# One transposition moved from a transfer to TensorE, one cast from ScalarE to VectorE, and other products cut in halves

## The chip, the cores and the metric

The kernel runs on one core of one Trainium2 chip. The metric is the device time of one execution in microseconds; lower is better. The core has five engines that run side by side and wait for each other by semaphores: TensorE (PE in the profile, its weight loads PEld), VectorE (DVE), ScalarE (ACT), GpSimd (POOL) and SyncE (SP). SyncE does no arithmetic: it issues transfers, in the order of the program. POOL issues transfers too, and each engine works its own list of instructions strictly in order.

## What is computed

A retention layer (attention with a decaying mask and no softmax) feeds a two-layer network with the Mish function. The reference, cut to what matters:

```python
# q, k, v: 8 batches x 8 heads x 576 positions x 64
scores = q @ k.T / sqrt(64)
gamma = 1 - 2 ** (-5 - head)
ret = (scores * where(i >= j, gamma ** (i - j), 0)) @ v
x = ret.transpose(0, 2, 1, 3).reshape(4608, 512)
h = x @ w_in                      # 512 -> 2048
g = h * tanh(softplus(h))         # Mish
out = g @ w_out                   # 2048 -> 512, float32
```

## The kernel before

The 4608 rows are cut into chunks of 128 positions of one batch (positions 512 to 575 of two batches share a chunk). There are 36 chunks; four make a tile of 512 columns, so there are nine tiles, t = 0 to 8. Chunks 0 to 7 (tiles 0 and 1) are the first 128 positions of each batch and go a way of their own. From chunk 8 (`N0`) on, each batch is worked through by running states: the sum of all earlier k-by-v products, kept per batch.

Each chunk from 8 on goes through these steps:

- `load(n)` (lines 266 to 281): POOL issues the transfers of q, k and v into `qkraw` (5 buffers) and `vraw` (7 buffers).
- `step_p(n)`, called "P" (line 291): two VectorE multiplications scale q and k by the decay and write `qks` in bf16.
- `step_v(n)`, "V" (line 298): v is scaled, on VectorE below chunk 18, on POOL from there on.
- `step_t(n)`, "T" (lines 301 to 319): q and k of the chunk are transposed into `qkT`. Below chunk `NPE` = 16, TensorE does it with eight 128x128 transposes into PSUM (line 310) and ScalarE copies the result out (line 316). From chunk 16 on, SyncE issues one transposing transfer (line 318).
- `step_s` (line 330), the scores of a pair of chunks, TensorE; `step_m` (line 336), the masking, VectorE.
- `states(n)` (line 385), the k-by-v products of a pair; `sum_up` (lines 408 to 416) adds them up on VectorE, and a cast to bf16 (line 419) waits in the list `casts` until `run(casts)` is called.
- `outputs` and `outputs_end` (lines 439 and 456), the retention's results; `outputs_copy` (line 468) brings them into the tile `xT`.

`visit(n)` does the TensorE part for a pair: the states and the scores of chunks n+2 and n+3, mixed with the outputs of chunks n and n+1. It is a stretch of 64x64 products, many instructions in a short time. `written` puts a waiting instruction on SyncE in the middle of each visit, so that transfers that SyncE issues later stand behind it.

The large products fill the time between visits. `g1(t, f)` makes one 128x512 block of the first layer (four products, line 504, and ScalarE's Mish, line 518, out of two PSUM buffers `hp`); `g2(t, i)` makes four products of the second layer. `product` (lines 502 to 510) does one such product as a whole, or, while the counter `halved[0]` is above zero, as two halves of 256 columns with a weight load each (line 509); the first and the last product of a sum are never halved.

The order of all this is written out by hand. A loop over u = 0 to 23 does the first layer of tile 1 and part of its second layer, with the steps of chunks 8 to 13 placed at fixed u. Then a loop over t = 2 to 9 and i = 0 to 15 goes on. In it, n = 4(t+1) + 2(i // 8) is the pair in work and w = i % 8 is the unit in its stage; below, "stage 14, unit 5" means n = 14 and w = 5. The visit of a pair stands in unit 6 of its stage. So tile 2 has stages 12 and 14, tile 3 has stages 16 and 18, and so on.

Transposing transfers and loads share the DMA engines. `hold(n)` (line 474) keeps them apart: POOL copies one element out of the transposed chunk n, so POOL, and every load behind it in POOL's list, waits until that transposition has landed. In stage 12 the lines around the change are:

```python
            if w == 7 and n + 4 == NPE:
                att(n + 5, "T")
                hold(n + 4)
                hold(n + 5)
                more_loads(n + 7)
```

Here `att(17, "T")` issues the transfer of chunk 17, the two holds wait for chunks 16 and 17, and `more_loads` goes on to chunk 18. Chunk 16 is transposed in unit 5 of stage 12. Chunks 18 and 19 are transposed, by transfers, in unit 7 of stage 14 and unit 0 of stage 16; visit 14 reads the scores' inputs of chunks 16 and 17, visit 16 those of chunks 18 and 19. In stage 14 the scaling "P" of chunk 18 stands in unit 4 and that of chunk 19 in unit 7.

Of the kernel before, what the change touches and what calls it, by code (L numbers as in the profile page):

```python
# [16 lines left out]
def kernel(  # L17
# [18 lines left out]
    nc = tc.nc  # L36
    B, H, S, D = q.shape
    assert (B, H, S, D) == (8, 8, 576, 64)
    P = 128
# [6 lines left out]
    NPE = 16  # L46
# [213 lines left out]
    def cast_k0(b, copy=nc.scalar.copy):  # L260
        k0[b] = first.tile([P, H, D], BF16, name="k0", bufs=3)
        copy(k0[b], k0r[b])
# [3 lines left out]
    def load(n):  # L266
        if n >= n_chunks:
            return
        b, c = chunks[n]
        qkr = io.tile([P, 2, H, D], F32, name="qkraw")  # L270
        vr = io.tile([P, H, D], F32, name="vraw", bufs=7)
        live[n] = {"qkr": qkr, "v": vr}
        for t, src in ((qkr[:, 0], q), (qkr[:, 1], k), (vr, v)):
            if c < 4:
                nc.gpsimd.dma_start(  # L275
                    out=t, in_=src[b, :, ds(P * c, P), :].rearrange("h p d -> p h d"))
            else:
                for e in range(2):
                    nc.gpsimd.dma_start(
                        out=t[ds(64 * e, 64)],  # L280
                        in_=src[b + e, :, ds(512, 64), :].rearrange("h p d -> p h d"))
# [19 lines left out]
    def step_t(n):  # L301
        flat = live[n]["qks"].rearrange("p i h d -> p (i h d)")
        qk = tr.tile([P, 2, NP, P], BF16, name="qkT", bufs=6)
        if n < NPE:
            if n in (N0 + 2, N0 + 4):
                tp = ps_st.tile([P, 2 * NP, P], BF16, name="st")
            else:
                tp = ps_sc.tile([P, 4 * NP, P], BF16, name="sc")[:, 0:2 * NP]
            for i in range(2 * NP):
                nc.tensor.transpose(tp[:, i, :], flat[:, ts(i, P)], ident)  # L310
            if n < N0 + NCH:

                nc.scalar.copy(qk[:, 0], tp[:, 0:NP])
                later.append(lambda: nc.scalar.copy(qk[:, 1], tp[:, NP:2 * NP]))
            else:
                nc.scalar.copy(qk.rearrange("p i n t -> p (i n) t"), tp)
        else:
            nc.sync.dma_start_transpose(out=qk.rearrange("p i n t -> p (i n) t"), in_=flat)
        live[n]["qk"] = qk
# [23 lines left out]
    def flush():  # L343
        while later:
            later.pop()()
# [6 lines left out]
    casts = []  # L352

    def behind(ins, others):

        sync = mybir.DependencyInfo(mybir.DependencyClass.Sync, mybir.DependencyReason.DATA)
        tc.add_manual_dep(ins.ins, others.ins.name, sync, reason="row halves and a bank")
# [8 lines left out]
    def states(n):  # L366

        if n >= n_chunks:
            return [], 0
        st = ps_sc.tile([P, 2, 2, NP, 64], F32, name="sc")  # L370
        whole = [b for b, c in chunks[n:n + 2] if c == 1]
        s0 = ps_st.tile([P, 2, NP, 64], F32, name="st")[:, 0] if whole else None

        made = []

        def part(x, j, p):
            r = ds(64 * j, 64)
            for e in range(2):
                hh = 4 * (p // 2) + 2 * e + p % 2
                if x is None:  # L380
                    ks, vs, to = k0[whole[0]][r, hh, :], v0s[whole[0]][r, hh, :], s0[ds(64 * e, 64), p, :]
                else:
                    ks, vs = live[n + x]["qks"][r, 1, 2 * p + e, :], live[n + x]["vs"][r, hh, :]
                    to = st[ds(64 * e, 64), j, x, p, :]
                ins = nc.tensor.matmul(to, lhsT=ks, rhs=vs, start=(x is not None or j == 0 and p == 0),  # L385
                                       stop=True, skip_group_check=True)
                made.append(ins)

        own = [x for x in range(2) if chunks[n + x][1] < 4]
        first_half, second_half = [None] * len(whole) + own, own + [None] * len(whole)  # L390

        def unit(i, seen=None):
            made.clear()
            for p in range(NP):
                part(first_half[i], 0, p)
                part(second_half[i], 1, p)
            if seen is not None:
                behind(made[0], seen)
            return made[-4:]

        def sum_up():
            new = tr.tile([P, 5, NP, 64], F32, name="total", bufs=2)
            lows = tr.tile([P, 5, NP, 64], BF16, name="ssb", bufs=2)
            k = 0
            for x in own:
                b, c = chunks[n + x]
                if c == 1:
                    nc.vector.tensor_copy(new[:, k], s0)
                    total[b], st_sb[b, c, 0] = new[:, k], lows[:, k]
                    k += 1  # L410
                for j in range(2):
                    if (c, j) == (3, 1):
                        st_sb[b, 4] = tr.tile([P, NP, 64], BF16, name="last", bufs=4)
                        nc.vector.tensor_tensor(st_sb[b, 4], st[:, j, x], total[b], op=OP.add)
                        continue
                    nc.vector.tensor_tensor(new[:, k], st[:, j, x], total[b], op=OP.add)  # L416
                    total[b], st_sb[(b, c, 1) if j == 0 else (b, c + 1, 0)] = new[:, k], lows[:, k]
                    k += 1
            casts.append(lambda: nc.scalar.copy(lows[:, 0:k], new[:, 0:k]))  # L419

        sums.append(sum_up)
        return [lambda seen=None, i=i: unit(i, seen) for i in range(len(first_half))], len(own)

    def run(jobs):
        while jobs:
            jobs.pop()()

# [42 lines left out]
    def hold(n):  # L472

        nc.gpsimd.tensor_copy(held[:, n % 2:n % 2 + 1], live[n]["qk"][:, 1, NP - 1, P - 1:P])  # L474
# [23 lines left out]
    halved = [0]  # L498
# [76 lines left out]
    def att(n, steps):  # L575
        if n >= n_chunks:
            return
        for step in steps:
            {"P": step_p, "V": step_v, "T": step_t}[step](n)

    dve, act, pool = nc.vector.tensor_copy, nc.scalar.copy, nc.gpsimd.tensor_copy
# [63 lines left out]
    for i in range(nF):  # L645
        for step in steps.get(i, "").split():
            n = int(step[1])
# [17 lines left out]
    def more_loads(upto):  # L665
        for _ in range(2):
            if queued[0] <= upto:
                load(queued[0])
                queued[0] += 1
# [5 lines left out]
    for u in range(24):  # L675
        j, w = divmod(u, 4)
        if u == 5:
            cast_k0(0)
        elif u == 14:
            cast_k0(1, dve)  # L680
        halved[0] = 2 if u < 5 else 0
        if u in ps:
            att(N0 + ps[u], "P")
        if u == 11:
            step_m(N0)
        if u in vs:
            att(N0 + vs[u], "V")
        if w == 0 and j > 0:
            if j < 5:
                if j == 4:  # L690
                    load_k0(2)
                load(N0 + j + 3)
            else:
                more_loads(N0 + j + PF)
                load_k0(3)
        if u == 10:
            units, early = states(N0)
            seen = written(units[0]())
            step_s(N0)
            units[1]()  # L700
            units[2](seen)
            run(sums)
        elif u == 16:
            att(N0 + 4, "P")
            visit(N0, ((ps_o, "ops"), (ps_h, "hp")), (act, act))
            run(sums)
        elif u == 22:
            visit(N0 + 2, ((ps_h, "hp"), (ps_h, "hp")), (act, dve))
        if u == 20:
            stores(act)  # L710
        if u in (13, 20):
            run(casts)
        if u in ts_:
            att(N0 + ts_[u], "T")
        stores()
        if u < nF:
            g1(1, u)
            flush()
        else:
            g2(1, u - nF)  # L720
# [3 lines left out]
    for t in range(2, nT + 1):  # L724
        for i in range(nF):
            n, w = NCH * (t + 1) + i // 8 * 2, i % 8
            if w == 2 and n in cast_at:
                cast_k0(cast_at[n])
            if w == 2:
                run(casts)  # L730
                halved[0] = {14: 10, 20: 24, 22: 24}.get(n, 0)
            if w == 6 and n < n_chunks:
                visit(n, ((ps_h, "hp"), (ps_h, "hp")), (act, dve), lambda: g2(t - 1, i))
            if w == 0:
# [3 lines left out]
                stores()  # L738
            if w in (0, 1) and n + 2 < NPE:
                att(n + 2 + w, "P")  # L740
            if w in ((4, 7) if n + 2 == NPE else (4, 5)) and n + 4 >= NPE:
                att(n + 4 + (w > 4), "P")
            if w in ((3, 4) if n + 2 < NPE else (0, 1)):
                att(n + 2 + (w in (1, 4)), "V")
            if w == 5 and 16 <= n < 24:
                f_state(1, n // 2 - 8, nc.vector)


            if w == 7 and n + 4 == NPE:
                att(n + 5, "T")  # L750
                hold(n + 4)
                hold(n + 5)
                more_loads(n + 7)
            if w == 4 and NPE < n + 2 < n_chunks:
                hold(n + 2)
                hold(n + 3)
# [69 lines left out]
```

## Time and profile before

| What | Value |
|---|---|
| median of three runs | 308.64 us (308.0 to 310.39) |
| the profiled execution's own time | 305.89 us |
| its span, first to last instruction | 304.2 us |
| mean granted TensorE clock | 0.994 |
| TensorE busy | 290.3 us, 95% of the span |
| VectorE, ScalarE, POOL busy | 135.4, 134.2, 137.9 us |
| transposing transfers | 20, landing 3.0 to 12.2 us after issue |

The profile is one execution. A group or timeline row names start and length in us, the engine, the line of the kernel, what is written and read, the shape and a count; the square bracket at the end tells how long the engine had stood idle before the row and what ended that wait. "issue" there means that no semaphore explains the wait. A row with SPq or POOL DMA is the issue of a transfer, not the transfer; a row "held<-qkT" on POOL is one `hold`. In the stretches, the busy time of each engine is followed by its number of instructions, then the granted clock, the mean share of time in which the 16 DMA engines were busy (it can pass 1, since packets overlap) and what they moved.

### The profile page before, as it was taken

Reading aid. Unit: us, or ns where it says so; the run is one execution under the profiler, and the core shown is the slowest. Engines: PE = TensorE matmul, PEld = TensorE weight load, DVE = VectorE, ACT = ScalarE, POOL = GpSimd, SP = SyncE. Lnnn points to the kernel's source line nnn. Section 1 sums busy time; section 2 is a strip of 40 time slices with the busy share of each in tenths; the row PEclk is TensorE's granted clock in tenths of the full one; section 3 lists DMA queues with packets and bytes.
Section 4 is the critical chain, followed back from the end, with each engine's and each line's share of the span. In section 5 each row is a group of like instructions: output and inputs, shape, how many; then the busy total and the mean of one; then the engine's idle time right before and its main releaser. Section 6 shows DMA issues by size and latency. Waiting matters only on the chain.

```text
span 304.2 us, 7939 instructions
## 1 busy us (share of the span) xinstructions
PE 290.3 (95%) x3456; PEld 159.5 (52%) x3494; DVE 135.4 (45%) x233; ACT 134.2 (44%) x220; POOL 137.9 (45%) x186
## 2 busy tenths in 40 slices
PE   8889999999989997999999999999899999999996
PEld 3456887555455543456656454545354544444443
DVE  3812547587963752554555545444443312011011
ACT  5656226785656532534353535343435343433300
POOL 8595856768408906591929345919240000000000
PEclk9999999999999997999999999999999999999999
DMA  7999999999986996989898989888922100110132
GB/s 150 204 206 205 205 241 230 333 220 204 253 158 168 213 163 177 217 194 190 190 194 135 198 170 228 183 166 152 196 72 69 39 34 34 37 34 34 37 102 71
DMA packets 41730, 47.96 MB, mean 158 GB/s; under 512 B 23904, under 2 KB 30560, under 8 KB 41696
## 3 DMA queue, kind: packets, MB, share of 16 engines
q0 software_dynamic: 14896, 32.25, 51.0%
q1 hardware_dynamic: 26656, 15.01, 24.0%
q8 instruction: 27, 0.44, 0.7%
q10 hardware_dynamic: 144, 0.20, 0.2%
q14 instruction: 7, 0.06, 0.1%
HBM read 38.80 MB, written 9.44 MB: 159 GB/s over the span
## 4 chain that ended last, share of the span: by engine, by line
PE 88%; DMA 6%; issue 2%; POOL 2%; ACT 1%; DVE 0%; POOLq 0%
PE hp L504 38%; PE ops L504 28%; PE hp L509 7%; PE ops L509 4%; DMA qkT<-qks 4%; DMA gT<-in_v_dram 2%; PE sc L330 2%; PE sc L385 1%; PE hp L456 1%; PE hp L559 1%; PE hp L439 1%; POOL gT L106 1%; PE st L509 1%; PE sc L310 1%; PE st L385 1%
## 5 line engine op out<-in xcount | busy, mean ns | idle before, releaser
L504 PE MATMUL hp<-xT,w_in_t 128*128 128x512 bf16 x495 | 127.3, 380 | 3.1 <-issue 1.1
L518 ACT ACTIVATE gT<-hp 128x512 bf16<-128x512 f32 x144 | 86.2, 599 | 96.0 <-PE hp L504 91.6
L504 PE MATMUL ops<-w_out_t,gT 128*128 128x512 bf16 x399 | 99.7, 381 | 2.0 <-issue 1.9
L504 PEld LDWEIGHTS <-w_in_t 128*128 128x128 bf16 x512 | 50.0, 98 | 54.8 <-issue 3.4
L504 PEld LDWEIGHTS <-gT 128*128 128x128 bf16 x468 | 44.7, 98 | 52.2 <-issue 2.0
L567 DVE COPY res<-ops 128x512 f32<-128x512 f32 x28 | 19.3, 691 | 79.8 <-PE ops L504 76.9
L291 DVE TENSOR_TENSOR qks<-qkraw,gqk 128x512 bf16<-128x512 f32 x56 | 36.9, 702 | 12.6 <-DMA qkraw<-in_k_dram 12.6
L474 POOL COPY held<-qkT 128x1 bf16<-128x1 bf16 x20 | 6.1, 304 | 71.4 <-DMA qkT<-qks 71.4
L468 DVE CAST xT<-hp 128x512 bf16<-128x512 f32 x13 | 9.0, 692 | 35.8 <-PE hp L456 33.1
L275 POOL DMA_DIRECT2D qkraw<-in_q_dram x24 | 21.4, 892 | 4.2 <-DMA vpair<-in_v_dram 1.5
L275 POOL DMA_DIRECT2D qkraw<-in_k_dram x24 | 21.2, 885 | 2.7 <-DMA w_out_t<-in_moe_w_out_dram 1.5
L275 POOL DMA_DIRECT2D vraw<-in_v_dram x24 | 21.2, 885 | 2.6 <-DMA vpair<-in_v_dram 1.5
L468 ACT CAST xT<-hp 128x512 bf16<-128x512 f32 x14 | 8.2, 587 | 31.6 <-PE hp L456 29.2
L509 PEld LDWEIGHTS <-gT 128*128 128x128 bf16 x184 | 17.6, 98 | 3.8
L298 POOL TENSOR_TENSOR vs<-vraw,gv 128x512 bf16<-128x512 f32 x18 | 18.9, 1077 | 1.2 <-PE hp L439 1.1
L509 PE MATMUL hp<-xT,w_in_t 128*128 128x256 bf16 x128 | 19.2, 272 | 0.0
L336 DVE TENSOR_TENSOR sm<-sc,mask 128x1024 bf16<-128x1024 f32 x14 | 17.0, 1216 | 1.4 <-PE sc L330 1.4
L416 DVE TENSOR_TENSOR total<-sc,total 128x256 f32<-128x256 f32 x40 | 16.9, 422 | 1.1
L509 PEld LDWEIGHTS <-w_in_t 128*128 128x128 bf16 x128 | 12.5, 98 | 7.7
L419 ACT CAST ssb<-total 128x768 bf16<-128x768 f32 (+3 forms) x14 | 12.9, 923 | 1.8 <-DVE total L416 1.7
L509 PE MATMUL ops<-w_out_t,gT 128*128 128x256 bf16 x100 | 13.1, 273 | 0.1
L504 PE MATMUL hp<-w_out_t,gT 128*128 128x512 bf16 x49 | 12.1, 379 | 0.1
(117 smaller groups left out, 249.7 us busy)
## 6 DMA issues: line engine op xcount, KB each, us to landing
out_dram<-res SPq DMA_DIRECT2D x31, 256.0 KB, 3.3
qkraw<-in_q_dram POOLq DMA_DIRECT2D x24, 256.0 KB, 6.9
qkraw<-in_k_dram POOLq DMA_DIRECT2D x24, 256.0 KB, 7.7
vraw<-in_v_dram POOLq DMA_DIRECT2D x24, 256.0 KB, 7.9
w_out_t<-in_moe_w_out_dram POOLq DMA_DIRECT2D x4, 512.0 KB, 11.7
k0r<-in_k_dram POOLq DMA_DIRECT2D x8, 256.0 KB, 5.5
w_in_t<-in_moe_w_in_dram POOLq DMA_DIRECT2D x3, 512.0 KB, 10.0
gT<-in_k_dram POOLq DMA_DIRECT2D x8, 128.0 KB, 6.4
```

Source lines behind the costliest of these rows:

```text
L275: nc.gpsimd.dma_start(out=t, in_=src[b, :, ds(P * c, P), :].rearrange("h p d -> p h d"))
L291: nc.vector.tensor_tensor(slots[:, :, y], heads[:, :, y], factors[:, :, y].unsqueeze(3).to_broadcast([P, NP, 2, D]), op=OP.mult)
L298: engine.tensor_tensor(vs, live[n]["v"], gv[:, c, :].unsqueeze(2).to_broadcast([P, H, D]), op=OP.mult)
L336: nc.vector.tensor_tensor(sm.rearrange("p e x n i -> p (e x n) i"), live[n]["sc"].rearrange("p e x n i -> p (e x n) i"), mask.unsqueeze(1) ...
L416: nc.vector.tensor_tensor(new[:, k], st[:, j, x], total[b], op=OP.add)
L419: casts.append(lambda: nc.scalar.copy(lows[:, 0:k], new[:, 0:k]))
L468: copy(xts[t][:, :, ds(P * s, 2 * P)].rearrange("p h (x j i) -> p j h x i", x=2, j=2)[:, j], both[j])
L474: nc.gpsimd.tensor_copy(held[:, n % 2:n % 2 + 1], live[n]["qk"][:, 1, NP - 1, P - 1:P])
L504: nc.tensor.matmul(to, lhsT=w, rhs=x, start=first, stop=last)
L509: nc.tensor.matmul(to[:, ts(j, n)], lhsT=w, rhs=x[:, ts(j, n)], start=False, stop=False, skip_group_check=True)
L518: nc.scalar.activation(gts[t][:, f, :], hp, AX.Mish)
L567: copy(ot, ops)
```

## The change

Four things are edited.

- `step_t` transposes chunk 17 on TensorE with a copy by ScalarE; chunk 16 and those from 18 on still go by transfers.
- The steps of chunk 17 are placed later: "P" in unit 2 of stage 14 (before: unit 5 of stage 12), "T" in unit 5 of stage 14 (before: unit 7 of stage 12). `hold(17)` is gone from stage 12.
- The waiting casts take the copying engine as an argument. At u = 13 it is VectorE (tile 2's first states, 128x1280); everywhere else it is ScalarE as before.
- The counter of halved products is set to 2 at u = 5 and 6 too, to 6 instead of 10 in stage 14, to 28 instead of 24 in stage 20, and to 10 instead of 24 in stage 22.

```diff
     def step_t(n):
...
-        if n < NPE:
+        if n < NPE or n == NPE + 1:
...
-            casts.append(lambda: nc.scalar.copy(lows[:, 0:k], new[:, 0:k]))
+            casts.append(lambda copy: copy(lows[:, 0:k], new[:, 0:k]))
...
-    def run(jobs):
+    def run(jobs, *how):
         while jobs:
-            jobs.pop()()
+            jobs.pop()(*how)
...
-        halved[0] = 2 if u < 5 else 0
+        halved[0] = 2 if u < 7 else 0
...
         if u in (13, 20):
-            run(casts)
+            run(casts, dve if u == 13 else act)
...
             if w == 2:
-                run(casts)
-                halved[0] = {14: 10, 20: 24, 22: 24}.get(n, 0)
+                run(casts, act)
+                halved[0] = {14: 6, 20: 28, 22: 10}.get(n, 0)
...
-            if w in ((4, 7) if n + 2 == NPE else (4, 5)) and n + 4 >= NPE:
+            if n + 2 == NPE and w == 2:
+                att(n + 3, "P")
+            if w in ((4, 7) if n + 2 == NPE else (4, 5)) and n + 4 >= NPE and (n + 4 > NPE or w == 4):
                 att(n + 4 + (w > 4), "P")
...
             if w == 7 and n + 4 == NPE:
-                att(n + 5, "T")
                 hold(n + 4)
-                hold(n + 5)
                 more_loads(n + 7)
+            if w == 5 and n + 2 == NPE:
+                att(n + 3, "T")
```

In the program that results, TensorE has 8 transposes more and 10 halved products fewer; VectorE's list has one cast more, ScalarE's one cast less and one copy of 128x1024 more, SyncE's one transfer less and POOL's one held copy less.

## The prediction

> **What bounds the kernel now.** The page comes first: where the time is, and who ends last.
>
> ```profile
> span 304.2 us, 7939 instructions
> ...
> PE 290.3 (95%) x3456; PEld 159.5 (52%) x3494; DVE 135.4 (45%) x233; ACT 134.2 (44%) x220; POOL 137.9 (45%) x186
> ...
> PE 88%; DMA 6%; issue 2%; POOL 2%; ACT 1%; DVE 0%; POOLq 0%
> ```
>
> TensorE is busy for 95% of the span and the other engines for half of it. So only two things can move the end: TensorE's own work, and the few places where it stands still. The second view is the chain that ended last, in order of time. DMA has 6% of it, and one piece stands in the middle of the kernel:
>
> ```profile
> 84.37 0.45 PE sc L310 x8
> ...
> 89.58 3.45 PE hp L504 x16
> ...
> 95.63 0.87 PE ops L509 x8
> ...
> 105.21 11.06 DMA qkT<-qks
> 117.61 1.49 PE ops L504 x3
> 119.10 2.20 PE hp L504 x8
> 121.30 0.86 PE ops L504 x4
> ```
>
> A transfer transposition issued at 105.21 us ends 11 us later, and TensorE goes on behind it. The third view is the timeline of TensorE around its visits (the stretches of 64x64 products). I quote the first row of the visits of chunks 12 and 16, and each row in them ahead of which TensorE stood still:
>
> ```profile
> 86.47 0.22 PE L385 MATMUL st<-v0s,k 64*64 64x64 bf16 x2
> ...
> 88.13 0.22 PE L330 MATMUL sc<-qkT 64*64 64x64 bf16 x3 [0.68 <-issue]
> ...
> 113.33 0.22 PE L385 MATMUL st<-v0s,k 64*64 64x64 bf16 x2
> ...
> 115.58 0.32 PE L330 MATMUL sc<-qkT 64*64 64x64 bf16 x16 [1.53 <-DMA qkT<-qks]
> ...
> 116.32 0.32 PE L330 MATMUL sc<-qkT 64*64 64x64 bf16 x16 [0.42 <-DMA qkT<-qks]
> ```
>
> Both visits hold the same kinds of work (with a k0 state). Visit 12 goes from 86.47 to 89.58, 3.11 us with a stall of 0.68, so 2.43 without; eight products (0.86 per four) then end at 4.2 us from its start. Visit 16 starts at 113.33 and its eight products end at 121.30: 7.97 us. Its two waits, 1.53 and 0.42 us, for the transposed chunks 18 and 19 explain half of the **3.8 us** lost. The rest is the clock, as the stretch behind the visit shows (columns: TensorE, its weight loads, DVE, ACT, POOL, granted clock, DMA share, GB/s):
>
> ```profile
> 118.00:120.50 2.50, 2.50 (x9) 0.97 (x8) 0.92 (x1) 0.03 (x1) 2.50 (x4) 0.61 0.65 161
> ```
>
> At 0.61 of the clock a product takes 0.27 to 0.5 us (rows 119.10 and 117.61 of the chain) instead of 0.22. The stall costs twice: while it lasts, and after it.
>
> **Why chunks 18 and 19 come late.** The queues' timeline and the stretches by DMA load:
>
> ```profile
> 83.96 4.69 SPq L318 DMA_TRANSPOSE qkT<-qks  x2
> ...
> 88.77 0.19 POOL L474 COPY held<-qkT 128x1 bf16<-128x1 bf16 x1 [9.09 <-DMA qkT<-qks]
> ...
> 92.32 0.54 POOL L474 COPY held<-qkT 128x1 bf16<-128x1 bf16 x1 [3.36 <-DMA qkT<-qks]
> ...
> 92.82 0.89 POOL L275 DMA_DIRECT2D qkraw<-in_q_dram  x1
> ...
> 103.30 7.34 SPq L318 DMA_TRANSPOSE qkT<-qks  x2
> ...
> 104.37 0.69 POOL L279 DMA_DIRECT2D vraw<-in_v_dram  x1 [0.26 <-DMA qkraw<-in_q_dram]
> ```
> ```profile
> 90.00:94.00 4.00, 4.00 (x21) 1.82 (x19) 3.34 (x7) 2.73 (x5) 1.68 (x3) 1.00 0.19 70
> 94.00:104.00 10.00, 9.79 (x178) 6.01 (x179) 4.87 (x8) 4.61 (x9) 10.00 (x13) 1.00 0.92 214
> 104.00:107.00 3.00, 3.00 (x16) 1.35 (x15) 1.79 (x6) 2.38 (x4) 2.72 (x4) 1.00 1.05 200
> 107.00:110.00 3.00, 3.00 (x15) 1.35 (x14) 1.29 (x3) 1.19 (x2) 0.12 (x1) 1.00 1.41 225
> ```
> ```profile
> DMA to landing us min/median/max: 3.0/5.9/12.2
> ```
>
> POOL's held(16) passes at 88.77; held(17) waits another 3.36 us for chunk 17's transfer, and only then, at 92.82, does POOL issue the loads of chunks 18 to 21. Meanwhile the DMA engines idle (share 0.19 from 90 to 94). The loads then fill them until about 109. Transpositions 18 and 19 are issued at 103.30 and 105.21, into full engines, and take 12.2 (the longest of all 20) and 11.1 us where the median is 5.9.
>
> **The change part by part.** The profiled execution took 305.89 us, its span 304.2, and the median shown is 308.64, or 2.75 above it; I take differences on the profile and subtract them from the median.
>
> *Chunk 17 off the transfer queue, held(17) gone.* SyncE and POOL each lose one instruction. held(16) waits only for chunk 16, issued at 83.96, 3.5 us ahead of 17, so it still passes at 88.77 and the next POOL instruction comes 3.55 us earlier (92.32 less 88.77), or 3.8 with the longer copy. All twelve loads' issues are back to back, so all move: the engines drain near 105.5 instead of 109. Transposition 18 stays at 103.3, since it stands on SyncE behind a result store that TensorE and DVE release. It then meets engines that drain 2 us later. With the median 5.9 us it lands at 109.2, and 19, issued at 105.2, at 111 to 113. TensorE asks for them at about 114.5 (113.33, plus the first units, plus 0.45 below). Both waits go, and with them the clock loss: **3.8 us** at most, 0 at least if the 12.2 us do not shrink. I take 3.8, because the slack is 1 to 3 us.
>
> *Chunk 17 on TensorE.* Eight transposes: 0.45 us on the chain (row 84.37 above), with nothing to hide them: **+0.45**. Their input, DVE's pair for chunk 17, moves from unit 5 of stage 12 to unit 2 of stage 14, behind the two value scalings of this row; ACT's copy and the scores that read chunk 17 follow:
>
> ```profile
> 84.94 1.02 ACT L316 COPY qkT<-sc 128x1024 bf16<-128x1024 bf16 x1
> ...
> 92.12 1.28 DVE L298 TENSOR_TENSOR vs<-vraw,gv 128x512 bf16<-128x512 f32 x2
> ...
> 99.56 0.50 PE L330 MATMUL sc<-qkT 64*64 64x64 bf16 x32
> ```
>
> The pair takes 1.28 us as well and ends near 94.7, unit 5 begins some 2.5 us ahead of the scores, near 97, and the copy, of 1.02 us, ends near 98.8, ahead of the scores at 99.56 plus 0.45. It delays one ACTIVATE by 1.02 us, behind which visit 14's second bank waits; TensorE has a unit of products in between. Cost 0; without that cover up to 0.6. The raw buffer that DVE now frees later is chunk 22's, loaded behind held(18) only.
>
> *The cast of 128x1280 from ACT to DVE.* The rows around unit 14 of stage 1:
>
> ```profile
> 64.22 1.27 ACT L419 CAST ssb<-total 128x1280 bf16<-128x1280 f32 x1
> ...
> 65.26 0.42 DVE L262 CAST k<-k0r 128x512 bf16<-128x512 f32 x1
> ...
> 66.04 1.02 PE L504 MATMUL hp<-xT,w_in_t 128*128 128x512 bf16 x4 [0.65 <-ACT gT L518]
> ...
> 67.92 0.20 PEld L330 LDWEIGHTS <-qkT 64*64 64x64 bf16 x14 [0.18 <-issue]
> ```
>
> ACT's 1.27 us stands ahead of the ACTIVATE that TensorE awaits for 0.65 us; that wait goes. On DVE the cast takes 0.42 (the 512 columns' row) to 1.05 us (0.42 x 1280/512; I take 1.0), and the k0 cast ends at 66.7 instead of 65.7, where the visit, at 66.99 now, would want it at 66.3. So 0.3 is left of 0.65. Behind it TensorE stops at 67.92 for its own code (next part), and that moment may not move. Bounds 0 and 0.65; I take **-0.2**.
>
> *Halves.* Eight halves take 0.87 us (95.63), four whole products 0.86 (121.30). Units 5 and 6 add four halved products, stage 14 loses four, 20 gains four, 22 loses fourteen: ten fewer, -0.03 us. What they change is the place of every later instruction. Three stops marked "issue" inside or behind visits have no semaphore; the weight loads up to them count:
>
> ```profile
> 0.00:88.10 88.10, 82.93 (x1106) 52.65 (x1118) 51.21 (x96) 51.79 (x85) 57.85 (x81) 1.00 1.08 222
> 0.00:216.05 216.05, 206.00 (x2753) 119.03 (x2782) 116.80 (x204) 105.87 (x173) 134.31 (x181) 0.99 0.98 198
> 0.00:67.91 67.91, 63.66 (x725) 41.75 (x734) 36.11 (x70) 39.70 (x67) 47.50 (x69) 1.00 1.09 222
> ```
> ```profile
> 216.09 0.38 PE L504 MATMUL hp<-xT,w_in_t 128*128 128x512 bf16 x1 [1.13 <-issue]
> ```
>
> 1118, 2782 and 734 differ by 384 and 1664 pairs of weight load and product: 3 and 13 times 128. So the code arrives in blocks of 256 instructions, and TensorE stops where a block comes late because a visit ran through the one before. In the new order the visits up to 12 lie 4 pairs later, 14 and 16 lie 8 later, 18 and 20 8 and 12, the later ones 0 to 2 earlier. The stop of 0.68 shrinks by up to four products' time (block asked for 0.87 us earlier), that of 1.13 by two (0.43): I take **-0.3 and -0.2**; bounds together are -1.8 (both gone) and +0.8 (a block needed 28 pairs, 6 us, behind visit 14 instead of 7.8 comes late).
>
> By the Trainium skill's "Runtime: NRT & Kernel Launch", section Instruction fetch mechanics, crossing such a block boundary is mostly hidden: the sum without these two terms gains 0.5 less. The 1.13 us above speaks against it.
>
> Sum: -3.8 + 0.45 - 0.2 - 0.3 - 0.2 = **-4.05**: 305.89 becomes 301.8, and 308.64 becomes **304.6**.
>
> **The rivals.**
> *(a) Chunks 18 and 19 still late.* For it: 103.30 is unchanged and the engines are full then; against it: they drain 3.8 us earlier. If the transposition itself needs 10 of its 12.2 us, it lands at 113.5 to 115, a wait of some 0.5 to 1 us is left and the clock still drops for a while: 2 of 3.8 saved, less 0.45, less 0.2 to 0.5 at the small stops: 306.8.
> *(b) Slower: the wait moves to the next visits.* held(18) and held(19) pass earlier, so the next pairs' loads start 4 us earlier too, and transpositions 20 to 23 meet them. The rows of number 21 and of the first products behind the visit that asks for it:
>
> ```profile
> 123.35 1.50 SPq L318 DMA_TRANSPOSE qkT<-qks  x1
> ...
> 133.81 0.81 PE ops L504 x3
> ```
>
> It would be issued near 119.5 and asked for near 129.5, 10 us later; from there on it decides, against a longest of 12.2. A late one costs 2.2 us of wait and 2.1 of clock; twice that, less 3.8, plus 0.45 is +5: 313.9. Against it: those loads are held behind 18 and 19 as before, so the whole pattern moves with TensorE.
> *(c) TensorE's transposes are dearer.* If one of 128x128 took 0.39 us here, eight would cost 3.12 instead of 0.45 and the sum would be -1.4: 307.3. The eight in 0.45 us speak against it. The Trainium skill's "VectorE: DVE Perf Modes", section The three transpose paths, gives those 390 ns for TensorE; its figure would eat most of this change's gain, and the trace does not bear it out.
>
> **How the numbers follow.** Forecast 0.66, (a) 0.20, (b) 0.11, (c) 0.03. About 1%, 3.1 us, is what a measurement of this kernel can tell from no change. The forecast's own range: 5.8 saved if every small stop goes too, 1.2 if code comes late: 302.8 to 307.4. Timed runs are 2.75 above the profile, and if part of that lies in the same stall, more is to be had: low 301.3. Up, (a) is held whole and (b) left out: 308.6. Faster by over 1%: 0.61 of the forecast and 0.03 of (a), 0.64; slower: 0.07 of (b); the rest, 0.29, within 1%.
>
> **What would show it.** In the new profile: one held copy near 88.8, the first load behind it near 89.2; transpositions 18 and 19 landing by 113; no wait for qkT at L330 and clock 1.00 behind visit 16; eight more L310 transposes and one L316 copy near 97; no wait for gT at 66. I am wrong if 18 or 19 still takes 10 us or more, if a wait for qkT shows at visits 18 or 20, or if a new "issue" stop of over 1 us stands behind visit 14.

## The result, and the profile after

The changed kernel is faster: 301.25 us in the median (300.05 to 307.34, 22 runs) against 305.22 (302.57 to 312.0, 22 runs) for the kernel before on the same chips. The ratio is **0.9917, with a 95% interval of 0.9891 to 0.9943**; a second comparison gave 0.9919 (0.9857 to 0.9982). That ratio leaves out the runs far above the fastest, more of them of the kernel before, so the ratio's 2.5 us are less than the 4.0 between the medians. Between the two profiled executions (305.89 and 300.05) lie 5.84; that of the kernel before is not one of the 22.

The page of the changed kernel, the same lines as before:

```profile
span 298.3 us, 7971 instructions
...
PE 291.2 (98%) x3492; PEld 158.0 (53%) x3492; DVE 138.1 (46%) x234; ACT 133.9 (45%) x220; POOL 136.6 (46%) x185
...
PE 91%; DMA 2%; DVE 2%; POOL 2%; issue 1%; ACT 0%; POOLq 0%
```

TensorE is as busy as before in a span 5.9 us shorter. DMA's share of the chain falls from 6% to 2%, which is what the first loads of the kernel take. The issues and the one remaining hold, from the timeline:

```profile
83.01 1.84 SPq L318 DMA_TRANSPOSE qkT<-qks  x1
...
88.08 0.19 POOL L474 COPY held<-qkT 128x1 bf16<-128x1 bf16 x1 [8.28 <-DMA qkT<-qks]
...
88.61 0.89 POOL L275 DMA_DIRECT2D qkraw<-in_q_dram  x1 [0.34 <-DVE sm L336]
...
95.35 0.61 PE L310 MATMUL sc<-ident,qks 128*128 128x128 bf16 x8
...
96.05 1.01 ACT L316 COPY qkT<-sc 128x1024 bf16<-128x1024 bf16 x1
...
101.90 5.41 SPq L318 DMA_TRANSPOSE qkT<-qks  x2
...
105.34 0.38 PE L504 MATMUL ops<-w_out_t,gT 128*128 128x512 bf16 x1 [0.47 <-issue]
...
108.58 0.19 POOL L474 COPY held<-qkT 128x1 bf16<-128x1 bf16 x1 [4.22 <-DMA qkT<-qks]
...
110.84 0.31 POOL L474 COPY held<-qkT 128x1 bf16<-128x1 bf16 x1 [2.07 <-DMA qkT<-qks]
```

One transposition and one hold stand where there were two. The load of chunk 18 is issued at 88.61 instead of 92.82, and POOL's holds for 18 and 19 pass at 108.58 and 110.84. The stretches show where the engines' work went (90 to 94 was at a DMA share of 0.19, 118 to 120.5 at a clock of 0.61):

```profile
90.00:94.00 4.00, 4.00 (x26) 2.35 (x25) 2.83 (x5) 2.78 (x6) 4.00 (x6) 1.00 0.87 241
...
107.00:110.00 3.00, 3.00 (x16) 1.37 (x14) 1.62 (x4) 1.19 (x3) 0.19 (x1) 1.00 0.70 140
...
118.00:120.50 2.50, 2.50 (x14) 1.15 (x12) 2.36 (x7) 1.19 (x2) 1.72 (x3) 1.00 1.04 218
```
```profile
DMA to landing us min/median/max: 3.1/5.7/9.4
```

The longest transposition fell from 12.2 to 9.4 us; chunks 18 and 19 themselves took 6.6 and 5.8 us, from 101.90 to 108.46 and from 105.00 to 110.79. The chain of the changed kernel, around chunk 17's transposes and visit 16, runs through TensorE:

```profile
95.51 0.45 PE sc L310 x8
...
103.36 1.51 PE ops L504 x7
104.87 0.47 issue
...
114.01 0.97 PE ops L504 x4
114.98 1.73 PE hp L504 x8
116.71 0.86 PE ops L504 x4
```

Visit 16 starts at 112.56, and its eight products end at 116.71: 4.15 us where the kernel before took 7.97.

The visits begin at fixed places of the program, so the difference of their start times tells in which stretch time was won (us; negative is a loss):

| Stretch, up to | Before | After | Won in the stretch |
|---|---|---|---|
| first visit (u = 10) | 59.21 | 58.80 | 0.41, ahead of every edit but a few halves, probably chance: the other profiles have 58.56 to 59.45 |
| visit 8, start | 66.99 | 66.17 | 0.41, the cast |
| visit 8, end | 68.56 | 67.58 | 0.16, the stop of 0.18 |
| visit 12, end | 88.53 | 86.69 | 0.86, mostly the stop of 0.68 |
| visit 14, start | 99.03 | 97.61 | -0.42, eight transposes |
| visit 16, start | 113.33 | 112.56 | -0.65, the new stop at 105.34 (0.47 idle; the product behind it starts 0.85 after the one ahead instead of 0.22) |
| visit 18, start | 132.45 | 127.86 | **3.82**, visit 16 and the clock behind it |
| visit 28, start | 208.57 | 203.96 | 0.02 |
| visit 30, start | 225.03 | 219.13 | 1.29, the stop of 1.13 |

Theory A, from the prediction: what cost time was that the loads waited for chunk 17's transfer. The rivals: the halves and the cast made the gain (B, C), or the engine time of that transfer did (D). A second theory is that TensorE's code comes in blocks of 256 instructions, and that halves move the stops.

### The profile page after: what moved, and what is told of

Same layout as the page of the kernel before. It is cut to its first block, busy times and chain, and to the rows that moved or that the text cites. A ratio compares the mean times of both kernels' runs of the same rounds, so it can differ in the third digit from the quotient of the medians.

```text
span 298.3 us, 7971 instructions
## 1 busy us (share of the span) xinstructions
PE 291.2 (98%) x3492; PEld 158.0 (53%) x3492; DVE 138.1 (46%) x234; ACT 133.9 (45%) x220; POOL 136.6 (46%) x185
## 4 chain that ended last, share of the span: by engine, by line
PE 91%; DMA 2%; DVE 2%; POOL 2%; issue 1%; ACT 0%; POOLq 0%
PE hp L504 39%; PE ops L504 31%; PE hp L509 7%; PE ops L509 3%; DMA gT<-in_v_dram 2%; PE sc L330 1%; PE sc L385 1%; PE hp L456 1%; PE hp L439 1%; PE hp L559 1%; POOL gT L106 1%; PE st L509 1%; PE sc L310 1%; PE st L385 1%; PE sc L190 1%
## 5 line engine op out<-in xcount | busy, mean ns | idle before, releaser
L504 PE MATMUL ops<-w_out_t,gT 128*128 128x512 bf16 x424 | 105.0, 379 | 0.5 <-issue 0.5
L504 PEld LDWEIGHTS <-gT 128*128 128x128 bf16 x478 | 45.5, 98 | 51.8
L291 DVE TENSOR_TENSOR qks<-qkraw,gqk 128x512 bf16<-128x512 f32 x56 | 39.4, 746 | 6.7 <-DMA qkraw<-in_k_dram 6.7
L474 POOL COPY held<-qkT 128x1 bf16<-128x1 bf16 x19 | 5.1, 267 | 64.2 <-DMA qkT<-qks 64.2
L509 PEld LDWEIGHTS <-gT 128*128 128x128 bf16 x164 | 15.7, 98 | 3.4
L419 ACT CAST ssb<-total 128x768 bf16<-128x768 f32 (+3 forms) x13 | 11.7, 897 | 3.6 <-DVE total L416 3.4
L509 PE MATMUL ops<-w_out_t,gT 128*128 128x256 bf16 x80 | 10.6, 273 | 0.0
```

The lines of the kernel that those rows point to most:

```text
L291: nc.vector.tensor_tensor(slots[:, :, y], heads[:, :, y], factors[:, :, y].unsqueeze(3).to_broadcast([P, NP, 2, D]), op=OP.mult)
L419: casts.append(lambda copy: copy(lows[:, 0:k], new[:, 0:k]))
L504: nc.tensor.matmul(to, lhsT=w, rhs=x, start=first, stop=last)
L509: nc.tensor.matmul(to[:, ts(j, n)], lhsT=w, rhs=x[:, ts(j, n)], start=False, stop=False, skip_group_check=True)
```

## The experiments

Unless said otherwise, ratios are to the kernel before, with 95% intervals. The texts of expectation count the stop at 216 us to "visit 24" and the one ahead of it to "visit 22"; they stand behind visits 28 and 24.

**One part alone.** e1 has the edits of chunk 17 without the cast and the halves.

```diff
-        if n < NPE:
+        if n < NPE or n == NPE + 1:
...
-                att(n + 5, "T")
                 hold(n + 4)
-                hold(n + 5)
                 more_loads(n + 7)
+            if w == 5 and n + 2 == NPE:
+                att(n + 3, "T")
```

> The kernel before with the edits of chunk 17 alone (transposed by TensorE, its scaling and transposition in stage 14, held(17) gone); cast and halves as before. Theory A (the wait on chunk 17's transfer made the loads late, and with them transpositions 18 and 19): visit 16 has no wait for qkT, full clock behind it, 3.8 us less there, 0.45 more for eight transposes. Block theory (code comes in blocks of 256 instructions): visit 12 stops for 0.7 as before, a stop of about 0.5 to 0.7 stands 28 pairs behind visit 14, and the stop behind visit 24 (1.13 before) grows by 8 pairs, 1.7 us, to some 2.8, because everything behind stage 14 lies 8 pairs later. Sum about 1 us faster than before (0.997). Rival B (the halves and the cast made the gain): visit 16 still waits, time 0 to 0.5 us above before.

Measured: 301.65 us in the median, ratio 0.995 (0.9907 to 0.9994). The medians lie 3.3 us apart and not 1; the ratio's 1.5 us agree with the forecast of 0.997. The profile of e1 was taken at a mean granted clock of 0.561 (503.5 us; another execution took 772.24), so e12 is the same kernel, run again for its profile.

> The kernel of e1 once more, for a profile at full clock. Block theory: a stop behind visit 14 as in the changed kernel, one in visit 12, and one of up to 2.8 us some 16 pairs behind visits 22 and 24, where the next block is needed 16 pairs behind the visit instead of 24. e1's 301.65 us say that not all of these are there; if none is, the place of the code decides only where blocks are already late.

It took 301.48 us. Its waits on TensorE above 0.3 us behind the start:

```profile
PE sc L330 <- issue: 1.0, 2, 0.5
...
PE hp L504 <- ACT gT L518: 0.6, 1, 0.6
PE ops L504 <- issue: 0.5, 1, 0.5
```

No wait for qkT is left, so the edits of chunk 17 by themselves remove it. The stops at 67.7 and 87.7 (1.0 together) and behind visit 14 (0.5) are those that were expected; the large ones behind visits 24 and 28 are not there.

e2 and e3 have the other two parts alone:

```diff
-            casts.append(lambda: nc.scalar.copy(lows[:, 0:k], new[:, 0:k]))
+            casts.append(lambda copy: copy(lows[:, 0:k], new[:, 0:k]))
...
-            run(casts)
+            run(casts, dve if u == 13 else act)
```

> The kernel before with the cast at u = 13 on VectorE alone. Theory: TensorE's 0.65 us wait for gT near 66 turns into a wait of 0.3 for the k0 cast, and the 0.18 stop in visit 8 grows by what is gained if code decides there; visit 16 waits as before. 0 to 0.4 us faster (0.9987 to 1.000). Rival: VectorE's list falls behind and the scaling of chunk 12 comes late for visit 10, 0.5 us slower (1.0016).

Measured: 305.18 us, ratio 1.0034 (0.9978 to 1.0089), no difference. The wait of 0.65 became one of 0.21 for the k0 cast, and the stop in visit 8 grew from 0.18 to 0.56, as expected. That the cast is worth nothing because code decides there is not shown, though: e4 and e12 stop there for 0.53 and 0.54 us with the cast on ScalarE, as before.

```diff
-        halved[0] = 2 if u < 5 else 0
+        halved[0] = 2 if u < 7 else 0
...
-                halved[0] = {14: 10, 20: 24, 22: 24}.get(n, 0)
+                halved[0] = {14: 6, 20: 28, 22: 10}.get(n, 0)
```

> The kernel before with the new counts of halves alone. Block theory: visits 8 to 12 lie 4 pairs later in the code, so the stop of 0.68 in visit 12 shrinks or goes; visits 14 to 18 lie as before; visits from 22 on lie 10 pairs earlier, so the next block is needed 34 pairs behind visit 24 instead of 24 and the stop of 1.13 there goes. The waits for qkT at visit 16 stay. 1 to 2 us faster than before (0.9935 to 0.997). Rival C (halves change nothing but 10 weight loads): same time (0.9999), stops as before.

Measured: 304.63 us, ratio 1.0048 (0.9998 to 1.0099). A miss: the stop in visit 12 went, the one behind visit 28 fell to 0.24, and nothing was gained. A new stop of 0.95 us without a semaphore stands in visit 22. The rows of TensorE's waits say why:

```profile
113.41 0.32 PE L330 MATMUL sc<-qkT 64*64 64x64 bf16 x16 [0.28 <-DMA qkT<-qks]
...
115.05 0.32 PE L330 MATMUL sc<-qkT 64*64 64x64 bf16 x16 [1.32 <-DMA qkT<-qks]
...
131.35 0.32 PE L330 MATMUL sc<-qkT 64*64 64x64 bf16 x16 [0.87 <-DMA qkT<-qks]
...
147.81 0.32 PE L330 MATMUL sc<-qkT 64*64 64x64 bf16 x16 [1.24 <-DMA qkT<-qks]
```

The clock did not drop behind visit 16, so TensorE came earlier to visits 18 and 20 and waited there too: 0.28 + 1.32 + 0.87 + 1.24 = 3.71 us of waits, against the 3.8 that the kernel before lost at one visit. e0, the kernel before once more, was run to see this.

> The kernel before once more, to see whether visit 16's loss is the same in another execution. Theory A: waits for qkT of 1.5 to 2 us at visit 16, and either a lower clock behind it or further waits at visits 18 and 20, as where only the halves were changed; time 303 to 306 us. Rival: no wait at visit 16, then the first profile was an odd one.

It took 308.49 us, above the 303 to 306 expected. Its waits on TensorE:

```profile
PE sc L330 <- DMA qkT<-qks: 3.1, 4, 1.6
PE hp L504 <- issue: 2.6, 1, 2.6
```

Waits for qkT stand at visits 16 (twice), 20 and 22. The stretches from visit 16 to visit 24 are 3.7 us longer than in the changed kernel (1.18 from 16 to 18, 0.79 from 20 to 22, 1.72 from 22 to 24). So the kernel before paid nearly the same sum in both profiled executions, in e0 in installments. The stop behind visit 28 was 2.57 us here with a drop of the clock behind it, 4.4 us in all; that is what lifts this execution above 305.89.

**The hold or the transfer.** e4 only takes `hold(17)` out of the kernel before; the transfer stays.

```diff
                 hold(n + 4)
-                hold(n + 5)
                 more_loads(n + 7)
```

> The kernel before without held(17): chunk 17 is still transposed by a transfer, but POOL's loads of chunk 18 no longer wait for it. Theory A (the wait is what costs): loads start near 89 instead of 92.8, transpositions 18 and 19 land by 113, no wait for qkT at visit 16, 3 to 3.8 us faster (0.988 to 0.990), unless 17 itself, now among the loads, lands behind 99.5 and visit 14 waits for it. Rival D (the transfer itself fills the engines): 18 and 19 land behind 114.5 all the same, and visit 16 waits 1 us or more; 0 to 1 us faster (0.997 to 1.000).

Measured: 301.24 us, against 304.98 for the kernel before and 301.65 for e1 in the same series of runs; the changed kernel had 301.25 in another. The ratio, 0.9949 (0.9903 to 0.9994), is a smaller gain than the 0.988 to 0.990 expected, and its interval reaches into rival D's 0.997 to 1.000, so the traces must decide. From the timeline:

```profile
85.18 4.72 SPq L318 DMA_TRANSPOSE qkT<-qks  x2
...
89.51 0.19 POOL L474 COPY held<-qkT 128x1 bf16<-128x1 bf16 x1 [8.80 <-DMA qkT<-qks]
...
103.73 5.14 SPq L318 DMA_TRANSPOSE qkT<-qks  x2
...
110.17 0.19 POOL L474 COPY held<-qkT 128x1 bf16<-128x1 bf16 x1 [5.37 <-DMA qkT<-qks]
...
112.47 0.48 POOL L474 COPY held<-qkT 128x1 bf16<-128x1 bf16 x1 [2.11 <-DMA qkT<-qks]
```

Both transpositions are issued from 85.18 on, the loads begin behind the first hold, and 18 and 19 are there by 112.47, ahead of visit 16's scores, and TensorE waits for none. Rival D, which has them land behind 114.5 and visit 16 wait 1 us or more, falls: the transfer may stay. e5 is the converse: chunk 17 on TensorE, and the loads late.

```diff
                 hold(n + 4)
-                more_loads(n + 7)
+            if w == 2 and n + 2 == NPE:
+                nc.gpsimd.tensor_copy(held[:, 1:2], gts[t][:, i - 1, NCH * P - 1:NCH * P])
+                more_loads(n + 5)
```

> The changed kernel (chunk 17 on TensorE), but POOL now also waits for the Mish block 9 of tile 2 before it loads chunk 18, so the loads start near 92.3 us as in the kernel before, though no transfer of chunk 17 runs. Theory A (the start of the loads decides): transpositions 18 and 19 land behind 113, TensorE waits for qkT at visits 16, 18 or 20, 2 to 4 us slower than the changed kernel: 303 to 305 us, 0.995 to 1.000 of before. Rival D (the engine time of chunk 17's transfer decides): no such wait, 301.2 us (0.99).

Measured: 308.04 us, ratio 1.0134 (1.0083 to 1.0184): slower than the kernel before, and 6.8 us above the changed one.

```profile
92.69 0.41 POOL L753 COPY held<-gT 128x1 bf16<-128x1 bf16 x1 [4.24 <-ACT gT L518]
...
93.20 0.89 POOL L275 DMA_DIRECT2D qkraw<-in_q_dram  x1
...
116.72 0.32 PE L330 MATMUL sc<-qkT 64*64 64x64 bf16 x16 [3.27 <-DMA qkT<-qks]
...
118.34 0.32 PE L330 MATMUL sc<-qkT 64*64 64x64 bf16 x16 [1.30 <-DMA qkT<-qks]
```

```profile
118.00:120.50 2.50, 1.82 (x67) 1.27 (x69) 1.44 (x2) 0.58 (x1) 1.80 (x3) 0.62 0.61 152
```

The loads started at 93.20, 0.4 us later than in the kernel before; the waits at visit 16 are 4.57 us, and the clock falls behind them. The direction is that of theory A; the size is above the 2 to 4 us expected. Chunks 18 and 19 took 13.95 and 13.77 us here; why 0.4 us of delay costs so much more than in the kernel before stays open. So the start of the loads decides, with or without chunk 17's transfer.

e9 asks what the transposition on TensorE is worth. It is the changed kernel with chunk 17 by a transfer without a hold, and 14 halves in stage 14, so that every visit's code lies as in the changed kernel.

> The changed kernel with chunk 17 transposed by a transfer again, in stage 12 as before, but without held(17); 14 halved products in stage 14, so that the code of every visit lies exactly as in the changed kernel. It asks what TensorE's transposition itself is worth. Theory A (only the hold mattered): 0.45 us of transposes saved, no wait for qkT: 300.8 us, 0 to 0.5 faster than the changed kernel. Rival D (the transfer's engine time matters too): 18 and 19 land 2 us later than in the changed kernel and visit 14 or 16 waits: 302 to 304.

Measured: 301.88 us, ratio 0.9926 (0.9881 to 0.997), the same as the changed kernel; the 0 to 0.5 us less that were expected do not show. Chunks 18 and 19 land at 109.17 and 111.55, 0.7 us later than in the changed kernel, and no visit waits for them. From the end of visit 12 to the start of visit 14 it takes 10.50 us instead of 10.92, the 0.42 of the transposes; the stop behind visit 14 is 0.90 instead of 0.47 and takes it back.

**Blocks of code.** e7 has the arithmetic of the changed kernel with more halves in stage 14.

```diff
-                halved[0] = {14: 6, 20: 28, 22: 10}.get(n, 0)
+                halved[0] = {14: 16, 20: 18, 22: 10}.get(n, 0)
```

> The changed kernel with 16 halved products in stage 14 instead of 6 (18 instead of 28 in stage 20, so that the code lies as before behind it). Same arithmetic. Block theory: the next block is needed 18 pairs behind visit 14 instead of 28, 2.2 us earlier, so the stop there grows from 0.5-0.65 to 2.6 us and stands ahead of the first product of the block; 303.3 us. Rival E (that stop is a place in the data flow, or halving hurts in itself): it stays 0.5 us, time within 0.3 of the changed kernel.

Measured: 303.63 us, ratio 0.9965 (0.9914 to 1.0016). The stop and the stretches up to it and behind it:

```profile
105.21 0.82 PE L504 MATMUL hp<-xT,w_in_t 128*128 128x512 bf16 x3 [2.47 <-issue]
```
```profile
0.00:105.15 105.15, 98.51 (x1359) 62.77 (x1374) 64.03 (x113) 59.98 (x99) 72.13 (x99) 1.00 1.03 219
105.00:108.00 3.00, 2.79 (x9) 1.03 (x9) 2.79 (x6) 1.83 (x3) 0.00 (x0) 0.65 1.33 136
108.00:110.50 2.50, 2.50 (x10) 1.02 (x9) 0.00 (x0) 0.17 (x1) 0.00 (x0) 0.74 1.20 130
```

2.47 us where 2.6 was expected, ahead of the weight load behind number 1374. The changed kernel stops at the same number, in another product:

```profile
0.00:105.30 105.30, 101.14 (x1373) 62.64 (x1374) 63.94 (x114) 61.10 (x101) 72.39 (x99) 1.00 1.04 219
```

1374 is 1118, the place of the stop in visit 12 before, plus 2 x 128. The block theory holds for the place. With ten more pairs ahead of it the stop is also far longer than the 0.14, 0.47 and 0.90 us that it has in the three profiles with the order of the changed kernel (e11, the changed kernel, e9). The stop costs more than itself: the clock falls to 0.65 and 0.74 behind it.

e6 goes the other way: no halves in stage 14, and the k0 cast ahead of the first states' cast.

```diff
-        elif u == 14:
-            cast_k0(1, dve)
...
+        if u == 13:
+            cast_k0(1, dve)
...
-                halved[0] = {14: 6, 20: 28, 22: 10}.get(n, 0)
+                halved[0] = {14: 0, 20: 34, 22: 10}.get(n, 0)
```

> The changed kernel with the k0 cast ahead of the cast of the first states on VectorE, and no halves in stage 14 (34 instead of 28 in stage 20, so that the code lies as before from there on). Block theory: the next block behind visit 14 is needed 34 pairs behind its end instead of 28, 1.3 us later, so the stop there goes; the wait of 0.33 for the k0 cast goes too. 0.8 us faster than the changed kernel, about 300.4 us. Rival: a stop appears elsewhere, 301.2 us.

Measured: 300.44 us, ratio 0.9884 (0.9829 to 0.9938). That is the time expected, but the interval reaches that of the changed kernel. In its profile the stop behind visit 14 and the wait for the k0 cast are gone.

**Both.** e10 is e6 with chunk 17 by a transfer without a hold; e11 is the changed kernel, run beside it.

> Chunk 17 by a transfer without held(17), the k0 cast ahead of the cast of the first states on VectorE, 8 halved products in stage 14 and 34 in stage 20, so that the code of every visit lies exactly as in the kernel without halves in stage 14 (e6). Theory: no wait for qkT, no stop behind visit 14, and 0.43 us of transposes less on TensorE: 0.4 us below e6, about 300.0 us, 0.987 of before. Rival: with chunk 17's transfer among the loads a block of code comes later and a stop of 0.4 us takes the gain back: 300.4 us.

> The changed kernel once more, to compare on the same chip. Expected 301.2 us, 1.2 us above e10, with a stop of 0.5 to 0.9 behind visit 14 in its profile; if its gain over before is what the profiles told, 0.986 to 0.988 of before, if what the first comparison told, 0.992.

e10: 300.26 us, ratio 0.9889 (0.9811 to 0.9966). e11: 300.94 us, 0.9919 (0.9857 to 0.9982). The difference between them lies inside the intervals. In e11's profile the stop behind visit 14 is 0.14 us and not the 0.5 to 0.9 expected: the same code at the same place stops for a different time in another execution, so the profile of e6 alone does not show what its missing halves are worth. The profile of e10 shows neither side's expectation but waits of the other kind:

```profile
PE sc L330 <- DMA qkT<-qks: 2.2, 3, 0.9
```

They stand at visits 18, 20 and 22. So in this execution transposition 21 is late again: it lands 10.6 us after its issue at 118.44. e6 with its longest transposition of 8.1 us had none; one profile each does not tell whether chunk 17's transfer is the reason.

## Why the prediction was right, point by point

*Chunks 18 and 19, 3.8 us.* Measured 3.82 between the two profiles, by the mechanism named: the loads 4.2 us earlier, the engines filled from 90 on, the holds passing at 108.58 and 110.84 (109.2 and 111 to 113 were forecast), no wait, full clock. e4 and e5 show that the start of the loads is the cause. That the moments fit so well is partly luck. Transposition 18 was issued at 101.90 and not at 103.3, since TensorE came 1.42 us earlier to visit 14, and the engines drained near 108 and not near 105.5 (share 1.19 from 105 to 108, 0.40 from 108 to 110.5). Rival (a) did not come, and e11, the second profile of the changed kernel, has no wait for qkT either. What the prediction did not see is that the 3.8 us are a debt and no property of visit 16: e0 and e3 pay nearly the same sum at three visits each. Rival (b) described this moving wait, but as the changed kernel's danger; it is how the kernel before works, and in e10 it came back. Why the ratio, 2.5 us, is below the debt stays open: the kernel before has executions at 302 us and below (300.32 the lowest, in the series of e1), which can hardly have paid it, and none of them was profiled.

*Chunk 17 on TensorE, +0.45.* Measured 0.42. ACT's copy took 1.01 us and hid, as worked out. Rival (c), by the dearer transposes, did not come: eight took 0.45 us again.

*The cast, -0.2.* 0.41 between the profiles, and a wait of 0.33 for the k0 cast where 0.4 was worked out (66.7 against 66.3). In e2 a longer code stop behind it took the gain back; whether the cast lengthened that stop is not shown.

*The code stops, -0.3 and -0.2.* This term was mis-sized: 0.86 + 0.16 and 1.29 were won and 0.65 lost behind visit 14, 1.66 net instead of 0.5. Most of it can't be put down to the halves. e4, with the code of the kernel before at its old places, has no stop behind visit 28 and none in visit 12 either; e12, where the block behind visit 28 is needed 8 pairs earlier, has none there. All the kernels with that stop load late, but e5 loads late too and has none. e0 stopped there for 2.57 instead of 1.13 us. So the place of a block decides where a stop can be and, as in e7, how long; but the same code at the same place stops for different times. The trace has the transfer itself, a packet of 16 KB in q8, the queue that the page of the profile calls instruction. For the block behind visit 28 it starts at 206.2 in e4, 1.0 us behind the visit's start; in the kernel before and in e0 it starts 4.7 and 6.2 us behind it, and the stop ends 2.8 us after the packet started in the one, 2.7 in the other. That other transfers on the DMA engines delay it is likely and not shown. The Trainium skill's "Runtime: NRT & Kernel Launch", section Instruction fetch mechanics, gives 256 instructions as the block size. The numbers 1118, 1374 and 2782 agree: they differ by multiples of 128 pairs. The same section calls the crossing "mostly hidden". At most visits here no stop shows, but at some one does: 2.47 us in e7.

*The sum.* -4.05 was forecast. The medians of 22 runs moved by 3.97; the ratio of 0.9917, put to the 308.64 shown before, gives 306.1, where 304.6 was forecast within 301.3 to 308.6. It lies within 1% by a little, where 0.64 was given to more than 1% and 0.29 to this. That -4.05 and 3.97 are so near is partly luck: between the profiles it was 5.84, since the stops gave 1.2 us more than forecast and the cast 0.2, and 0.41 lay ahead of the edits. For the runs that the ratio compares, the first term is the one that was probably too large, since it was read from an execution that paid the debt in full; this is argued and not shown. The 1.2 us at the lower end of the forecast's own range do not follow from its terms either, which leave 1.95 at the least (3.8 - 0.45 - 0.6 - 0.8).

## What to carry to other kernels

A wait on a queue that issues loads is paid where the loads are needed, here 20 us later, and it may be paid at several places, so add up the waits of all of them before you price one. Before you replace a transfer by engine work, try to leave out only the order that it imposed: one line less gave 301.24 us where the whole change gave 301.25. Where a stretch of many short instructions stands ahead, count instructions: where a block boundary falls cost 2.47 us in e7, and the clock behind it.

## What the runs showed of the hardware

In these profiles the drop of the clock goes with the length of the idle time. It came behind waits of 1.53 + 0.42 us (0.61 in the next stretch), 1.33 + 0.79 in e2, 3.27 + 1.30 in e5, 2.47 in e7 and 2.57 in e0. It did not come behind 0.28 + 1.32 in e3, whose mean clock is 1.000, nor behind 1.59 in e0 at visit 22. Each time the clock stood at 0.50 for 3.4 us and was full again: from 116.5 to 119.9 us in the kernel before, from 118.6 to 122.0 in e5. So a drop costs about 1.7 us of TensorE's work, an estimate from these two numbers; with the 1.95 us of waits that is nearly all of the 3.8 us lost there.

The Trainium skill's "TensorE: Matmul & The Clock Gate", Part 1, states a half-rate clock after an idle window of about 3.4 us that runs freely. The half rate agrees with the 0.50 that e5 shows from 119 to 122 us, but 2.47 us of idle time were enough in e7.

A transposing transfer beside loads is not slow in itself: chunk 17's took 3.7 us in e4 (88.67 to 92.39) while the loads began, against 12.2 us for chunk 18's in the kernel before, behind loads issued ahead of it.
